# First batch's loads in written order, four weight tiles and two units' loads behind a copy to x, and other idle products, in a linear-attention and mixer kernel

## The chip, the cores and the metric

The kernel runs on one core of one Trainium2 chip. The metric is the device time of one execution in microseconds, the median of several runs. A core has a matrix engine (TensorE, here PE; its weight loads are shown apart as PEld), a vector engine (VectorE, DVE), an activation engine (ScalarE, ACT), a general engine (GpSimd, POOL) and a queue engine (SyncE, SP) that issues the DMA transfers. Each engine works through its own instructions in order; they wait for each other through semaphores.

## The reference

Two blocks follow each other. The first is a gated linear attention (hgrn2) over 4 batches, 8 heads, 768 steps and head dimension 48. The second is a token mixer of low rank and a channel mixer, on x of 4 x 768 x 384:

```python
f = 1.0 / (1.0 + np.exp(-f_logit))
state = np.zeros((B, H, D, D))
for t in range(S):
    state = f[:, :, t, :, None] * state + np.einsum('bhd,bhe->bhde', k[:, :, t], v[:, :, t])
    y[:, :, t] = np.einsum('bhd,bhde->bhe', q[:, :, t], state)
x = y.transpose(0, 2, 1, 3).reshape(B, S, H * D)
h = x.transpose(0, 2, 1) @ U @ V                 # U: 768 x 32, V: 32 x 768
u = x + h.transpose(0, 2, 1)
out = u + np.maximum(u @ w_ch1, 0.0) @ w_ch2     # w_ch1: 384 x 1536, w_ch2: 1536 x 384
```

q, k, v and f_logit are float32. The weights U, V, w_ch1 and w_ch2 come as float64, and the kernel turns them into float32 itself.

## The kernel before

The attention is cut into units of two heads: unit n is batch n // 4, head pair n % 4, so units 0 to 3 are the first batch. `factored_path` does the work; `general_path` behind it is compiled but not taken with these inputs. The sequence of a unit is cut into 12 chunks of 64 steps. A unit has a front (`prepare`: the logarithms or gates, the keys, the queries) and a rear (`attend`: `kept`, `spread`, `states`, `scan`, `scores`, `mask`, `read`, `inner`). `inner` ends with an ACT copy (L948) that puts the unit's 96 columns into `x_tiles[b]`. A mixer of a batch follows its attention (class `Mixer`); in the first batch the low-rank part is done in two pieces of columns: `done` holds the columns of units 0 to 2, `rest` those of unit 3.

The weights come in blocks of 128 x 384 words of 64 bits: `weights[0:3]` are U and V's two parts, `weights[3:15]` are the twelve blocks of w1, then twelve of w2. Each has a `start` (its DMA, L82), `halves` (two ACT instructions, L91 and L92) and `join` (three DVE instructions, L98 to L100, and an addition on POOL, L101). The first six blocks of w1 (`FIRST = 6`) land two by two in three tiles named zw, which `place` (L634) takes from the pool zp; those after them land in four rotating buffers named w_raw. A call of `loads[i]` starts a later block and converts block i.

The loads of q, k, v and f are issued by `load(n, ...)` on SP's queue (L544 to L572). Six issues fetch f, k and q of a unit of the first six, and three its v. Units up to 5 share two sets of buffers (`late` for even ones, `other` for odd), so that unit n + 2 waits for unit n's readers. A load's semaphore is one of eight used in turn.

What sets the order: PE's instructions stand as they are written, in the whole path. For the first batch and most of the second (L1026 to L1115) DVE and ACT do so as well; SP and POOL are in an order that the framework's scheduler makes. In that stretch the loop of L1043 runs over the four units of the first batch. It lists the pieces of unit n's rear, of unit n - 1's rear and of unit n + 1's front, calls them, and then issues loads: unit 3's f and unit 2's k, q, v and the first three weights after n = 0; unit 3's k, q, v and six blocks of w1 after n = 1; units 4 and 5 after n = 2 and 3. Three more weights follow at L1070. Behind the loop come the first mixer's low-rank products, from `low_rank_of(done)` (L1077) to `mix_of(rest)` (L1090), then `turn` (L261, the transposes of x, tile put) and `ch1` (L273, tile pz), the first large products. `ch1` writes one of two PSUM buffers, which an ACT relu (L283) frees.

Two helpers issue products whose results nobody reads: `busy(n)` (L1031) n products of 128 x 384, and `warm(n)` (L214) n products of 128 x 128. POOL fills `starts` (a plane of `other`) and both `fz` with zeros (L1093 to L1095); the second batch's gates need them.

Of the kernel before, what the change touches and what calls it, by code (L numbers as in the profile page):

```python
# [10 lines left out]
F32 = mybir.dt.float32  # L11
U32 = mybir.dt.uint32
U64 = mybir.dt.uint64
# [5 lines left out]
WP = 384  # L19
# [92 lines left out]
def ahead_by(n, loads):  # L112


    def call(i):
        if i + n < len(loads):
            loads[i + n][0]()
        loads[i][1]()

    return [lambda i=i: call(i) for i in range(len(loads))]  # L120
# [367 lines left out]
def factored_path(ctx, tc, q, k, v, f_logit, moe_U, moe_V, moe_w_ch1, moe_w_ch2, out, ok):  # L488
# [4 lines left out]
    nc = tc.nc  # L493
    B, H, S, D = q.shape
    P = nc.NUM_PARTITIONS
# [4 lines left out]
    HP = H // 2  # L500
# [4 lines left out]
    NFC = FF // P  # L505
# [17 lines left out]
    zp = ctx.enter_context(tc.tile_pool(name="zp", bufs=3))  # L523
# [21 lines left out]
    def load(n, *names):  # L545

        b, hp = divmod(n, HP)
        for nm in names:
            if nm == "v":
                v_tiles[n] = three.tile([P, NBL, 2, D], F32, name="v_nat")  # L550
            for par in range(2):
                head = src[nm][b, 2 * hp + par]
                if nm == "v" and par:

                    for s in range(2):
                        nc.sync.dma_start(
                            out=v_tiles[n][(1 - s) * C : (2 - s) * C, :, par, :],
                            in_=head.rearrange("(c s p) d -> s p c d", s=2, p=C)[s],
                        )
                    continue  # L560
                if nm == "v" or n < TURNED:
                    dst = v_tiles[n] if nm == "v" else nat[n % 2][nm]
                    nc.sync.dma_start(out=dst[:, :, par, 0:D], in_=head.rearrange("(c p) d -> p c d", p=P))
                    continue
                head = head.rearrange("(c i) d -> i c d", i=NB)
                for part in range(2):
                    p0 = par * PAD + part * NB
                    n_ch = min(NB, D - part * NB)
                    nc.sync.dma_start(  # L569
                        out=raw[n % 2][nm][p0 : p0 + NB, :].rearrange("p (c d) -> p c d", d=NB)[:, :, 0:n_ch],  # L570
                        in_=head[:, :, part * NB : part * NB + n_ch],
                    )  # L572
# [35 lines left out]
    starts = other[:, 3, :]  # L608
    fz = [const.tile([P, S + 1], F32, name=f"fz{i}") for i in range(2)]
# [17 lines left out]
    weights = [take_in(U, moe_U.rearrange("(c p) r -> p c r", p=P))]  # L627
    weights += [take_in(*pair) for pair in by_rows(V, moe_V, R)]
    early = len(weights)
    w1_rows = moe_w_ch1.rearrange("(c p) f -> p c f", p=P)  # L630

    spare = []
# [7 lines left out]
    FIRST = 6  # L640
# [128 lines left out]
    x_tiles = {}  # L769

    def mixer(b):
        return Mixer(tc, b, x_tiles[b], U, V, w1, w2, sums if b else None, ident, blocks, out, two, three, zp, ps_big, ps_mm,
                     b == 0, z_all, room if b >= B - 2 else None, FEWER - (b - B + 2) * NCH // 4)
# [184 lines left out]
    def front(n, *names):  # L958

        if n >= NU:  # L960
            return []
        if n not in ahead:
            ahead[n] = dict(zip(("gates", "keep", "keys", "read_back", "queries"), prepare(n)))
        return [ahead[n].pop(nm) for nm in names]

    def rear(n, *names):

        if not 0 <= n < NU:
            return []
        if n not in here:  # L970
            here[n] = dict(zip(("kept", "states", "scan", "scores", "read", "inner", "mask", "spread"), attend(n)))
        return [here[n].pop(nm) for nm in names if nm in here[n]]
# [9 lines left out]
    def steps(first, last):  # L982

        for n in range(first, last):
            yield from joined(rear(n - 2, "inner"), rear(n - 1, "scores"), rear(n, "kept"))
            if n + 1 < NU and n + 1 not in v_tiles:
                load(n + 1, "v")
            yield from front(n + 1, "gates", "keep", "keys")
            yield from joined(rear(n - 1, "read"), rear(n, "states", "scan"))
            yield from front(n + 1, "read_back", "queries")  # L990
            if n + 1 == last:
                yield from rear(n - 1, "inner")
                if n + 2 < NU:
                    load(n + 2, "v")

    def attention(pieces, portions, todo):

        fill = Fill(todo, portions)
        for piece in pieces:
            fill()  # L1000
            piece()
        fill.rest()
# [23 lines left out]
    with tc.manual_schedule(engines={nc.vector.engine, nc.scalar.engine}):  # L1026


        idle = ps_mm.tile([P, 512], F32, name="idle", tag="mm")

        def busy(n):  # L1031
            for _ in range(n):
                nc.tensor.matmul(idle[:, 0:DM], lhsT=ident, rhs=ends[:, 0:DM], start=True, stop=True)  # L1033

        busy(2)
        for piece in front(0, "gates", "read_back", "keep"):
            piece()
        load(2, "f")
        load(1, "k", "q", "v")
        loads = ahead_by(early + FIRST, weights)  # L1040
        halves, join = [[w[i] for w in weights[:early]] for i in (2, 3)]
        done, rest = slice(0, 2 * (HP - 1) * D), slice(2 * (HP - 1) * D, DM)
        for n in range(HP):  # L1043
            last = n + 1 == HP
            pieces = rear(n - 1, "scan", "mask") + front(n, "keys")
            if last:
                pieces += join[:1]
            elif n < 2:
                pieces += [lambda: busy(2)]
            pieces += rear(n, "spread") + rear(n - 1, "read") + rear(n, "kept")  # L1050
            if last:
                pieces += halves[1:2] + front(n, "queries") + rear(n - 1, "inner") + join[1:2] + rear(n, "states")
                pieces += halves[2:] + rear(n, "scores")
            else:
                pieces += rear(n - 1, "inner") + front(n + 1, "gates") + front(n, "queries") + rear(n, "states", "scores")
                pieces += (halves[:1] if n + 2 == HP else []) + front(n + 1, "read_back", "keep")
            for piece in pieces:
                piece()
            if n == 0:
                load(3, "f")  # L1060
                load(2, "k", "q", "v")
                for load_w in weights[:early]:
                    load_w[0]()
            elif n == 1:
                load(3, "k", "q", "v")
                for load_w in weights[early : early + FIRST]:
                    load_w[0]()
            else:
                load(n + 2, "f", "k", "q", "v")
        for load_w in weights[early + FIRST : early + FIRST + early]:  # L1070
            load_w[0]()

        m = mixer(0)
        low_rank_of, added_up_of, mix_of, warm = m.some
        for piece in rear(n, "scan", "mask") + join[2:]:
            piece()
        low_rank_of(done)  # L1077
        warm(2)
        loads[early]()
        for piece in rear(n, "read"):  # L1080
            piece()
        added_up_of(done)
        for piece in rear(n, "inner"):
            piece()
        mix_of(done, range(0, NBL - 2, 2))
        low_rank_of(rest)
        mix_of(done, range(NBL - 2, NBL, 2))
        added_up_of(rest)
        warm(2)
        mix_of(rest)  # L1090
        warm(2)
        loads[early + 1]()
        nc.gpsimd.memset(starts, 0.0)  # L1093
        for t in fz:
            nc.gpsimd.memset(t, 0.0)  # L1095
        loads = loads[early + 2 :]

        start = m.before[3:5] + m.firsts[0:1] + m.before[5:]

        EARLY = 6  # L1100
        second = chain(front(HP, "gates", "keep", "keys", "read_back", "queries"), steps(HP, 2 * HP + 1))
        for i, (_, piece) in enumerate(start + m.firsts[1:]):
            piece()
            if loads:
                loads.pop(0)()
            if i >= EARLY:
                next(second)()
        for f in loads:
            f()
        n = len(m.seconds) // (NBL // 2)  # L1110
        todo, after = m.seconds[:-n], m.seconds[-n:]

        attention(second, 12 + 10 * HP - (len(start) + len(m.firsts) - 1 - EARLY), todo)
        m = start_mixer(1, after)
        for f in to_sum:  # L1115
            f()
# [5 lines left out]
    pieces = beside(steps((B - 1) * HP + 1, NU + 1), 10 * (HP - 2), [lambda i=i: sum_of_w(i) for i in range(len(W_SUMS))])  # L1122
# [374 lines left out]
```

## Time and profile before

| | |
|---|---|
| runs | 488.84, 484.67, 487.88 us; median 487.88 |
| profiled execution, device time | 486.5 us |
| its span (first to last instruction) | 484.7 us |
| mean granted clock of TensorE over the span | 0.987 |
| busy: PE, PEld, DVE, ACT, POOL | 466.6, 402.8, 344.1, 179.8, 39.3 us |
| chain that ended last: PE, DVE, ACT, no releaser ("issue"), SP, DMA | 79%, 10%, 3%, 3%, 2%, 2% |

Times in the profile count from the span's first instruction. A line of a timeline has the start, the time taken, engine, source line, operation, tiles written and read, shape and count; in brackets stands the idle time of the engine before it and what ended it. A line of the chain has start, time and what ran; "issue" is time in which the engine waited for nothing that the profile shows. A line of a stage table has the stretch, its length, the busy time of PE, PEld, DVE, ACT and POOL with instruction counts, the granted clock of PE, the DMA engines' busy share and what they moved in GB/s. A product of float32 is recorded twice.

The stretch around the change ends at about 56 us, where the first product of `ch1` starts (56.05 us). From there to about 108 us PE is in `ch1` almost without a break, beside the second batch's first units.

### The profile page before, as it was taken

To read this page: it belongs to the slowest core of one execution; us is meant where nothing else is said; L and a number is where in the kernel's file an instruction comes from. 1 tells how busy PE (TensorE), PEld (TensorE's weight loads), DVE (VectorE), ACT (ScalarE), POOL (GpSimd) and SP (SyncE) were. 2 spreads that over 40 slices of the span, in tenths; PEclk is the share of its full clock that TensorE was granted. 3 is DMA by queue.
4 is the path that set the end of the run, shared out by engine and by line. 5 is a ranking of instruction groups with operands and counts; after the bars stand their busy time and mean duration, and the time that the engine had idled before them with its cause. 6 is when DMAs were issued, how large, how long until landed. Compare 5 with 4: busy or idle time off the path is not lost.

```text
span 484.7 us, 12802 instructions
## 1 busy us (share of the span) xinstructions
PE 466.6 (96%) x5563; PEld 402.8 (83%) x5563; DVE 344.1 (71%) x552; ACT 179.8 (37%) x333; POOL 39.3 (8%) x51
## 2 busy tenths in 40 slices
PE   6997999999999899999999999999999999999995
PEld 4885888886666468799899888899979999999995
DVE  2556579778999847666766655997896886858642
ACT  4683575664444313433342304543221311112200
POOL 3013145444000000000000000000000000000000
PEclk9998699999999999999999999999999999999999
DMA  9979975757687613152516300100000000000001
GB/s 145 158 163 245 182 186 132 162 144 93 102 122 114 102 41 43 26 74 50 85 26 108 50 16 18 28 3 20 17 1 1 33 2 18 18 0 34 1 33 40
DMA packets 158680, 34.36 MB, mean 71 GB/s; under 512 B 149206, under 2 KB 157078, under 8 KB 158614
## 3 DMA queue, kind: packets, MB, share of 16 engines
q1 hardware_dynamic: 158614, 33.44, 37.3%
q8 instruction: 46, 0.75, 0.7%
q14 instruction: 20, 0.16, 0.1%
HBM read 28.70 MB, written 4.72 MB: 69 GB/s over the span
## 4 chain that ended last, share of the span: by engine, by line
PE 79%; DVE 10%; ACT 3%; issue 3%; SPq 2%; DMA 2%; POOL 1%; DVEq 0%; POOLq 0%
PE pw L327 26%; PE pz L273 22%; PE pp L425 11%; PE sc L837 2%; PE y L942 2%; PE y L924 2%; PE put L261 2%; DVE late L759 2%; PE po L298 2%; PE pt L678 1%; PE pt L705 1%; DVE added L907 1%; SPq L569 1%; PE pt L864 1%; PE idle L1033 1%
## 5 line engine op out<-in xcount | busy, mean ns | idle before, releaser
L273 PE MATMUL pz<-uT,w 128*128 128x256 f32 x504 | 114.1, 382 | 1.1 <-ACT z_all L283 1.1
L273 PEld LDWEIGHTS pz<-uT,w 128*128 128x128 f32 x504 | 93.9, 190 | 14.3 <-ACT z_all L283 1.5
L327 PE MATMUL pw<-w,z_all 128*128 128x192 f32 x216 | 37.7, 329 | 0.0
L327 PE MATMUL pw<-zw,w_raw 128*128 128x192 f32 x216 | 37.3, 327 | 0.0
L327 PEld LDWEIGHTS pw<-zw,w_raw 128*128 128x128 f32 x216 | 35.2, 190 | 0.7 <-DVE w_raw L197 0.6
L327 PEld LDWEIGHTS pw<-w,z_all 128*128 128x128 f32 x216 | 35.0, 190 | 0.7
L101 POOL TENSOR_TENSOR w<-w_y,w_r 128x384 int32<-128x384 int32 x24 | 31.5, 1312 | 45.9 <-DVE w_y L100 38.6
L283 ACT ACTIVATE z_all<-pz 128x512 f32<-128x512 f32 x33 | 19.7, 597 | 34.6 <-PE pz L273 34.6
L425 PE MATMUL pp<-v_nat,late 128*128 128x128 f32 x224 | 28.8, 275 | 0.0
L425 PEld LDWEIGHTS pp<-v_nat,late 128*128 128x128 f32 x224 | 27.0, 192 | 0.0
L418 ACT ACTIVATE other<-other 128x512 f32<-128x512 f32 x18 | 11.3, 631 | 40.0 <-DVE other L197 40.0
L298 PE MATMUL po<-w,z_all 128*128 128x384 f32 x72 | 24.9, 493 | 1.2 <-DVE o L197 1.2
L912 ACT COPY st<-added 128x576 f32<-128x576 f32 x12 | 14.7, 1222 | 30.5 <-DVE added L907 30.5
L298 PE MATMUL po<-w,zw 128*128 128x384 f32 x72 | 25.3, 496 | 0.0
L741 DVE TENSOR_TENSOR_SCAN late<-fz,late 128x768 f32<-128x768 f32 x12 | 21.1, 1755 | 4.0 <-ACT fz L736 3.6
L850 DVE TENSOR_TENSOR A<-sc,causal 128x768 f32<-128x768 f32 x16 | 15.1, 945 | 10.5 <-PE sc L837 10.5
L298 PEld LDWEIGHTS po<-w,z_all 128*128 128x128 f32 x72 | 13.3, 190 | 10.1 <-DVE o L197 1.8
L298 PEld LDWEIGHTS po<-w,zw 128*128 128x128 f32 x72 | 13.1, 190 | 9.7 <-issue 1.2
L759 DVE TENSOR_TENSOR_SCAN late<-fz,other 128x768 f32<-128x768 f32 x12 | 21.0, 1747 | 0.2
L98 DVE TENSOR_SCALAR w_y<-w_y 128x384 f32<-128x384 f32 (+3 forms) x27 | 13.1, 487 | 10.6 <-ACT w_y L91 10.4
L197 DVE TENSOR_TENSOR x<-x,pu 128x768 f32<-128x768 f32 (+3 forms) x14 | 11.2, 835 | 12.9 <-PE pu L248 7.8
L924 PEld LDWEIGHTS y<-st,qT 48*64 48x64 f32 x704 | 13.7, 137 | 7.7 <-issue 5.4
(214 smaller groups left out, 855.0 us busy)
## 6 DMA issues: line engine op xcount, KB each, us to landing
w_raw<-in_moe_w_ch_dram SPq DMA_DIRECT2D x18, 384.0 KB, 3.5
out_dram<-o SPq DMA_DIRECT2D x24, 192.0 KB, 2.0
v_nat<-in_v_dram SPq DMA_DIRECT2D x16, 144.0 KB, 3.6
v_nat<-in_v_dram SPq DMA_DIRECT2D x32, 72.0 KB, 3.6
zw<-in_moe_w_ch_dram SPq DMA_DIRECT2D x6, 384.0 KB, 6.0
late<-in_f_logit_dram SPq DMA_DIRECT2D x10, 96.0 KB, 3.0
late<-in_k_dram SPq DMA_DIRECT2D x10, 96.0 KB, 2.7
late<-in_q_dram SPq DMA_DIRECT2D x10, 96.0 KB, 2.7
```

Source lines behind the costliest of these rows:

```text
L98: nc.vector.tensor_scalar(f, f, SMALLEST, LARGEST, ALU.max, ALU.min)
L101: nc.gpsimd.tensor_tensor(dst.bitcast(I32), shaped(y.bitcast(I32)), shaped(r), ALU.add)
L273: nc.tensor.matmul(pm[:, i * 2 * P : (i + 1) * 2 * P], lhsT=w1[:, m, o : o + P], rhs=uT[a][:, m, :], start=(m == 0), stop=(m == NDC - 1))
L283: nc.scalar.activation(z[a, c][:, k : k + 2, :].rearrange("p i t -> p (i t)"), pm, AF.Relu)
L298: nc.tensor.matmul(pm, lhsT=z[a, i // NI][:, i % NI, s * P : (s + 1) * P], rhs=w2[:, i, :], start=(i == 0), stop=(i == NFC - 1))
L327: nc.tensor.matmul(pm[:, n * HM : (n + 1) * HM], lhsT=lhs[:, i, :], rhs=rhs[:, i, :], start=(i == 0), stop=(i == NI - 1))
L425: nc.tensor.matmul(pm[:, i, r * P : (r + 1) * P], lhsT=room["w"](wn)[:, r * P : (r + 1) * P], rhs=x_node(a, xn), start=((xn, wn) == of[0]) ...
L741: nc.vector.tensor_tensor_scan(backwards(X, S - 1, S), backwards(f, S, S), backwards(ends, S - 1, S), 0.0, ALU.mult, ALU.add,)
L759: nc.vector.tensor_tensor_scan(Y, f[:, 0:S], starts, 0.0, ALU.mult, ALU.add)
L850: nc.vector.tensor_tensor(T["A"], sc[:, :, 0 : NBL * C].rearrange("p h (c i) -> p h c i", i=C), causal.unsqueeze(1).unsqueeze(1).broadcast ...
L912: nc.scalar.copy(st, states.rearrange(by_e, c=NCH))
L924: nc.tensor.matmul(o(c % 2, par, c // 2), lhsT=T["q"][rows[par], chunk[c]], rhs=T["st"][rows[par], c, :], start=(c <= 2), stop=False, skip ...
```

## The change

Five edits, all in `factored_path`:

- SP's instructions of the first batch stand in written order (`written`, closed behind the last loads of that stretch). The f of unit 2 thereby goes ahead of unit 1's k, q and v, and unit 3's f ahead of unit 2's.
- Only two of the six blocks of w1 are issued after n = 1. The other four are issued by `held`, called in the last iteration behind `rear(n - 1, "inner")`, the last copy but one to x. `held` takes the two zw tiles and has ACT copy one column of x into each, so that the DMAs into them cannot start before that copy; then it issues unit 4's loads.
- Unit 5's loads and the next three weights are issued behind the last conversion of V.
- `starts` and the two `fz` are filled by DVE behind the first block of w1, in place of POOL.
- `warm(2)` before `mix_of(rest)` is gone, and the one behind it is `warm(3)`.

In the changed program's order, v of unit 6 stands on SP behind unit 7's f, k and q; before it stood ahead of unit 6's f.

```diff
+        written = ExitStack()
+        written.enter_context(tc.manual_schedule(engines={nc.sync.engine}))
         busy(2)
...
+        def held():
+            for i in range(2, FIRST, 2):
+                t = zp.tile([P, NFC // 2, 2 * P], F32, name="zw").rearrange("p i t -> p (i t)")
+                nc.scalar.copy(t[:, 0:1], x_tiles[0][:, 0, 0:1])
+                spare.extend([t.bitcast(U64)[:, 0:WP], t.bitcast(U64)[:, WP : 2 * WP]])
+            for load_w in weights[early + 2 : early + FIRST]:
+                load_w[0]()
+            load(HP, "f", "k", "q", "v")
...
-                pieces += halves[1:2] + front(n, "queries") + rear(n - 1, "inner") + join[1:2] + rear(n, "states")
+                pieces += halves[1:2] + front(n, "queries") + rear(n - 1, "inner") + [held] + join[1:2] + rear(n, "states")
...
                 load(3, "k", "q", "v")
-                for load_w in weights[early : early + FIRST]:
+                for load_w in weights[early : early + 2]:
                     load_w[0]()
-            else:
-                load(n + 2, "f", "k", "q", "v")
-        for load_w in weights[early + FIRST : early + FIRST + early]:
-            load_w[0]()
...
         for piece in rear(n, "scan", "mask") + join[2:]:
             piece()
+        load(HP + 1, "f", "k", "q", "v")
+        for load_w in weights[early + FIRST : early + FIRST + early]:
+            load_w[0]()
+        written.close()
         low_rank_of(done)
         warm(2)
         loads[early]()
+        nc.vector.memset(starts, 0.0)
+        for t in fz:
+            nc.vector.memset(t, 0.0)
...
         added_up_of(rest)
-        warm(2)
         mix_of(rest)
-        warm(2)
+        warm(3)
         loads[early + 1]()
-        nc.gpsimd.memset(starts, 0.0)
-        for t in fz:
-            nc.gpsimd.memset(t, 0.0)
```

## The prediction

> **What bounds the kernel now.** I read the page's slices first. TensorE (PE) is near 96% busy, and its granted clock dips in one place only, the fifth slice, 48 to 61 us:
>
> ```profile
> PE   6997999999999899999999999999999999999995
> ...
> PEclk9998699999999999999999999999999999999999
> DMA  9979975757687613152516300100000000000001
> ```
>
> The change stays in the first 60 us (the first batch's attention, then the first mixer's low-rank part). So next comes the chain of waits there (start, us, what):
>
> ```profile
> 40.77 0.64 PE y L924 x18
> 41.41 2.01 issue
> 43.42 0.89 PE y L924 x24
> ...
> 53.79 2.33 PE put L261 x12
> 56.13 2.75 PE pz L273 x12
> ```
>
> Inside one run of equal products PE stops for 2.01 us with no releaser. Then the stage table (us, busy of PE, PEld, DVE, ACT, POOL, clock, DMA share, GB/s):
>
> ```profile
> 40.00:42.00 2.00, 1.35 (x22) 1.04 (x22) 1.90 (x6) 1.03 (x3) 0.51 (x2) 1.00 1.09 339
> 42.00:44.00 2.00, 0.58 (x25) 0.58 (x26) 0.74 (x2) 0.00 (x0) 1.00 (x1) 1.00 1.15 204
> 46.00:48.00 2.00, 2.00 (x22) 0.96 (x22) 0.70 (x2) 0.64 (x1) 0.00 (x0) 0.50 0.64 116
> 56.00:58.00 2.00, 2.00 (x11) 1.77 (x10) 1.30 (x4) 2.00 (x5) 0.12 (x1) 1.00 0.75 130
> ```
>
> DMA is full when PE stops, and from 45.52 to 55.76 us (the clock record) PE runs at half clock. That is why 12 transposes (put) take 2.33 us there; 18 take 1.97 at 178.92.
>
> The instruction packets on queue q8 tell the stop. [...] The one [...] starts at 41.10 and takes 1.12. In its way:
>
> ```profile
> 33.19 4.00 SPq L82 DMA_DIRECT2D zw<-in_moe_w_ch_dram  x6
> ```
>
> Six weight tiles of 384 KB, landing until 44.14. So the stage's bound is a late instruction fetch, then the slow clock behind it. From 59.5 to 108 us the chain is dense pz products, and from 113 to 168 it is DVE's; a gain at 56 us should travel through both.
>
> [...]
>
> **The change, part by part.** The sum is against the profiled execution: span 484.7, device time 486.5. The median of the three runs is 1.4 above that.
>
> *Four tiles held back.* Only two weight tiles now go out at 33.2; the other four wait in SP's queue for two ACT copies behind the x copy that ends at 37.70, so they issue from about 38.2 and move data from about 39.7 (issue to first landing is some 3 us). [...] the 2.01 stop goes.
>
> *The clock.* [...] Then I walk the chain at full-clock prices. y ends 41.9, ph 42.5 (0.68), y L942 43.4, eight pu 44.4, the x copy at 44.2 frees ph at 44.4, four pu 45.4, two ACT h copies (0.24 each) with ph between them 46.0, twelve pu 47.0, idle products 47.7. The last x additions (0.41 each) end at 48.0 and 48.4; then DVE's three steps of weight block 1 (0.36, 0.36, 0.56) 49.7, POOL's addition 50.7, first pz 50.75 instead of 56.05: **-5.3**, of which 2.0 is the stop.
>
> *Idle products.* Two pairs become one of three: two products fewer. The pair before mix_of(rest) cost 1.23 on the path (50.31 to 51.54); the three behind it hide under the additions and POOL's block 1. This is inside the -5.3. [...]
>
> *Memsets from POOL to DVE.* On POOL they ran at 4.03, 30.21 and 37.27 (to 38.02, before V's conversion at 38.58): their going gains nothing. On DVE three of 768 columns cost 0.70 each by this row, 2.1 in all, ahead of the x additions, where DVE now idles 4.53:
>
> ```profile
> 1.66 0.70 DVE L606 MEMSET late<- 128x768 f32 x1 [0.22 <-issue]
> ...
> 47.30 1.42 DVE L197 TENSOR_TENSOR x<-x,pu 128x576 f32<-128x576 f32 x2 [4.53 <-PE pu L248]
> ```
>
> With the stop gone the cover shrinks to about 1.5: DVE is free at 45.0 to 45.4 and the first additions are up to 1.0 late, but the last ones wait for PE at 47.0. Cost 0 to 0.5; I take 0.1.
>
> *Two ACT copies of one column*, about 0.15 each (the row of seen, L931, 0.15): added, the scan (1.36) and A shift by 0.3; y L924 had 0.9 of room behind the scan. Cost 0 to 0.3; I take 0.
>
> *Loads in written order.* f of unit 2 now stands before k and q of unit 1, and waits for unit 0's log sums (PE, 8.8 us); k and q (four issues), then v (three), are queued behind it. k of unit 1 landed at 13.60; two landings later (0.9 each) it is 15.4, just under its transposes at 15.59. q lands near 18.3, needed 20.17. f of unit 2 comes 4 us sooner, but DVE's 0.72 wait for it is not on the chain: ACT gets there only at 20.84, behind the x copy. The next batch of three swaps likewise with 1 us to spare. From -0.2 to +0.4; I take 0.
>
> *Behind the held tiles* on SP stand units 4 and 5 (f, k, q, v, nine issues each), then the weight tiles. DMA idles some 2 us at 38, and tile three lands about 0.9 later than its 40.36; all later loads shift by about that. The next weight block was issued at 55.84; it should land near 60.4. ACT reaches it 5.3 sooner than here:
>
> ```profile
> 63.20 0.58 ACT L91 ACTIVATE w_y<-w_raw 128x384 f32<-128x384 f32 x1 [0.45 <-POOL w L101]
> ```
>
> that is at 57.9, and waits 2.5. Behind it in ACT's order is a relu copy of pz that frees one of two PSUM buffers; PE has one more pz (2.6) to run, so little is passed on. v of unit 6 moves behind unit 7's loads (from 58.5 to about 110) and is needed at 127.7: nothing. From 0 to +2.5; I take +0.3.
>
> *The next fetch*, [...] now meets four tiles and f of unit 4. [...] No row shows it so placed: 0 to +2; I take +0.2.
>
> **Sum:** -5.3 +0.1 +0.3 +0.2 = -4.7: span 480.0, device 481.8, and with the median's 1.4 **483.2**. The shift has to live through the DVE stage to 168 us, whose order is unchanged.
>
> **The rivals.**
> (a) *Both stop and slow clock go* (forecast): 480.5 to 484.5. For: the fetch's lag stands alone among its neighbours and beside the tiles. Chance 0.52.
> (b) *Only the stop goes*: [...] Then the slow stretch costs its 3.3 again and the gain is 2.0 to 2.5: 485.5. Chance 0.16.
> (c) *Nothing*: the fetch is late for another reason (it lags as much with two tiles), or ACT's wait for the next weight block gives all back: 486.5 to 488.5. Against: two tiles are moved by 38. Chance 0.14.
> (d) *Slower*: [...] The stop of 2 to 3 comes back, and the half clock of 10.24 falls on dense pz products, where it costs 5.1 instead of 3.3; with the late weight block's 2.5 that is -5.3 +2.5 +5.1 +2.5 = +4.8 at worst, +3 in the middle: 491, up to 493. For: DMA is fuller there than now. [...] Chance 0.18.
>
> **How the numbers follow.** A measurement of this kernel tells about 1% from no change: 483.0 and 492.8. (a) straddles the lower bound; its small costs (+0.6 in all) are upper guesses, so I put 0.37 of its 0.52 below, and with the tail of (b), 0.03, faster is 0.40. Slower by over 1% is the far end of (d) and of the late weight block, 0.14; the rest, 0.46, is within 1%. The range 480.3 to 489 leaves out the ends of (a) and the upper half of (d).
>
> **What would show it.** Right: no "issue" of 2 us near 41; clock 1.00 throughout 10 to 60; the q8 packet near 37 to 39; first pz near 50.7; the first w_raw conversion on ACT ended by a DMA. Wrong: a stop of PE inside put; a clock of 0.50 anywhere from 45 to 70; pz later than 54; or an early gain that is gone by 108 or 168 us.

## The result, and the profile after

The changed kernel takes **484.09 us** (median of 20 runs, 482.98 to 485.23), the kernel before beside it 485.58 (20 runs, 482.35 to 488.84): a ratio of 0.996, 95% interval 0.994 to 0.998. That is within 1%, inside the forecast range, and 0.9 above the forecast of 483.2. The profiled execution has a span of 482.0 against 484.7 before, and 483.7 us of device time against 486.5. Medians are over all runs; two of the 22 runs of w_first_no_hold and two of hold_two's (both below) are slow, over 1.5% above the fastest of their kernel (the profiled execution of w_first_no_hold is one), and without them these two medians are 484.76 and 482.78.

The page's slices of the kernel after (PE's busy tenths, its granted clock, the DMA engines):

```profile
PE   6999989999999899999999999999999999999995
PEclk9999999999999999999999999999999999999999
DMA  9977985658787521153426200100000000000001
```

The dip of the clock in the fourth and fifth slice is gone. The chain of waits through the same stretch (start, us, what):

```profile
41.22 1.17 PE y L924 x43
42.39 0.68 PE ph L232 x2
...
47.48 0.86 PE ph L217 x6
48.35 0.67 PE put L261 x6
49.02 0.02 issue
49.04 0.81 ACT uT L262
49.85 0.14 issue
49.98 2.83 PE pz L273 x12
...
57.74 4.31 DMA w_raw<-in_moe_w_ch_dram
```

The y products run through in one piece: the stop of 2.01 us is gone, and the first pz starts at 49.98 instead of 56.05. But the chain then leaves PE and follows a weight block's DMA. The stage table (same columns as before) shows both ends:

```profile
40.00:42.00 2.00, 1.50 (x46) 1.37 (x46) 1.93 (x6) 1.30 (x3) 0.00 (x0) 1.00 0.74 213
42.00:44.00 2.00, 2.00 (x70) 1.44 (x66) 1.82 (x4) 0.58 (x3) 1.03 (x2) 1.00 1.02 333
46.00:48.00 2.00, 1.67 (x19) 1.41 (x19) 2.00 (x4) 1.13 (x3) 0.00 (x0) 1.00 0.77 144
...
62.00:64.00 2.00, 0.34 (x2) 0.32 (x3) 1.22 (x3) 1.87 (x5) 0.00 (x0) 1.00 1.09 351
```

From 42 to 44 PE is busy throughout (before: 0.58). From 62 to 64 it is busy for 0.34 of 2.00, where before had:

```profile
62.00:64.00 2.00, 2.00 (x11) 1.77 (x10) 1.93 (x5) 1.55 (x4) 0.99 (x1) 1.00 1.00 255
```

The timeline tells why:

```profile
57.74 6.76 SPq L82 DMA_DIRECT2D w_raw<-in_moe_w_ch_dram  x5
...
62.13 0.54 ACT L91 ACTIVATE w_y<-w_raw 128x384 f32<-128x384 f32 x1 [5.44 <-DMA w_raw<-in_moe_w_ch_dram]
...
63.66 5.45 PE L273 MATMUL pz<-uT,w 128*128 128x256 f32 x24 [1.76 <-ACT z_all L283]
...
73.31 2.86 PE L273 MATMUL pz<-uT,w 128*128 128x256 f32 x12 [0.96 <-ACT z_all L283]
```

ACT waits 5.44 us for the seventh block of w1. The relu of pz (L283, 63.02) stands behind that block's two conversions, so PE, with both PSUM buffers full, stops for 1.76. Because ACT is late, so are the second batch's gates on it (L728, 67.65) and DVE's scan behind them (L741, 70.76 to 72.51); the relu at 72.67 stands behind a copy that waits for the scan, and PE stops again for 0.96.

Against the kernel before, PE's work stands like this: first pz -6.07 us, the pz products up to 61 us the same, those at 66 us -4.04, from 76 us to the end -2.8. So **6.07 us were gained and 3.3 given back** between 61 and 76 us. The stage itself gained a little more: in this execution PE stood some 0.5 us behind before's from 9 to 38 us, its clock being full only from 9.12 us on (before: 7.97).

### The profile page after: what moved, and what is told of

Read it like the earlier page. It is cut to its first block, busy times and chain, and to the rows that moved or that the text cites. A ratio compares the mean times of both kernels' runs of the same rounds, so it can differ in the third digit from the quotient of the medians.

```text
span 482.0 us, 12801 instructions
## 1 busy us (share of the span) xinstructions
PE 462.7 (96%) x5561; PEld 399.8 (83%) x5561; DVE 345.3 (72%) x555; ACT 179.8 (37%) x335; POOL 36.3 (8%) x48
## 4 chain that ended last, share of the span: by engine, by line
PE 70%; DVE 13%; ACT 4%; DMA 4%; SPq 3%; issue 3%; POOL 1%; DVEq 0%; POOLq 0%; ACTq 0%
PE pw L327 26%; PE pz L273 16%; PE pp L425 12%; PE y L942 2%; DVE late L759 2%; PE sc L837 2%; PE y L924 2%; SPq L569 2%; PE po L298 2%; PE put L261 1%; PE pt L705 1%; DVE added L907 1%; PE pt L864 1%; PE idle L1033 1%; DVE late L741 1%
## 5 line engine op out<-in xcount | busy, mean ns | idle before, releaser
L283 ACT ACTIVATE z_all<-pz 128x512 f32<-128x512 f32 x33 | 19.7, 597 | 32.7 <-PE pz L273 32.6
L741 DVE TENSOR_TENSOR_SCAN late<-fz,late 128x768 f32<-128x768 f32 x12 | 21.1, 1756 | 4.0 <-ACT fz L736 3.6
L418 ACT ACTIVATE z_all<-z_all 128x512 f32<-128x512 f32 x12 | 7.6, 632 | 32.8 <-DVE z_all L197 32.8
L892 ACT COPY added<-ds 48x576 f32<-48x576 f32 (+1 forms) x28 | 17.8, 635 | 3.3 <-PE ds L885 3.2
```

What stands on the lines that cost most here:

```text
L283: nc.scalar.activation(z[a, c][:, k : k + 2, :].rearrange("p i t -> p (i t)"), pm, AF.Relu)
L418: nc.scalar.activation(dst, dst, AF.Relu, scale=float(SIGNS[n]))
L741: nc.vector.tensor_tensor_scan(backwards(X, S - 1, S), backwards(f, S, S), backwards(ends, S - 1, S), 0.0, ALU.mult, ALU.add,)
L892: nc.scalar.copy(added[r, 1:].rearrange("p (e c s) -> p e c s", c=NBL, s=2), ds[r, :, 0 : NBL * D].rearrange("p s (c e) -> p e c s", e=D),)
```

## The experiments

Fetch times below are the starts of the instruction packets on queue q8 (46 in before's trace, 0.75 MB) and count from the zero of the chain. On this zero the fetch that the prediction put at 41.10 stands at 40.80. The experiments were measured in three sets, each beside the kernel before, and the changed kernel only in the set of the result. The lowest runs of before in these four sets are 482.35, 482.74, 482.47 and 482.05, so a difference under about 0.7 us between sets is not read as an effect here. Medians of kernels that lose the clock differ more between sets (before: 485.58 to 487.60).

### What gives 3.3 us back

**w_first**: the three next weight blocks go ahead of unit 5's nine issues on SP.

```diff
-        load(HP + 1, "f", "k", "q", "v")
         for load_w in weights[early + FIRST : early + FIRST + early]:
             load_w[0]()
+        load(HP + 1, "f", "k", "q", "v")
         written.close()
```

> The changed kernel, with three weight blocks (six to eight of w1) issued ahead of unit 5's loads and no longer behind them. Theory A (the changed kernel gains 6.1 us at the first pz and gives 3.2 back because ACT waits 5.4 us for the next weight block's DMA): ACT's wait for w_raw near 57 to 62 us is under 1 us, PE has no stop of 1.8 us near 62, the first pz stays at 50 us, and the time falls by 2.5 to 3.2 us, to 481 (ratio to before 0.990). Theory B (the conversion chain of ACT, DVE and POOL is the limit there anyway, or unit 5's loads become late in turn): the time stays within 1 us of 484.1, and another wait ends where the DMA's ended.

Measured: 481.11 us (6 runs), ratio to before 0.989 (0.984 to 0.994). The first pz is at 49.76, and behind it, in the timeline:

```profile
56.94 0.57 ACT L91 ACTIVATE w_y<-w_raw 128x384 f32<-128x384 f32 x1 [0.46 <-POOL w L101]
...
66.62 0.56 ACT L91 ACTIVATE w_y<-w_raw 128x384 f32<-128x384 f32 x1 [1.42 <-DMA w_raw<-in_moe_w_ch_dram]
...
71.02 2.86 PE L273 MATMUL pz<-uT,w 128*128 128x256 f32 x12 [0.93 <-ACT z_all L283]
```

ACT's wait is no longer for the block but for POOL (0.46), and PE has no stop at 63. What is left is the fourth block, still issued behind unit 5: 1.42 on ACT, 0.93 on PE.

**f_first**: all four blocks ahead of unit 4's k, q, v and of unit 5.

```diff
             for load_w in weights[early + 2 : early + FIRST]:
                 load_w[0]()
-            load(HP, "f", "k", "q", "v")
+            load(HP, "f")
...
         for load_w in weights[early + FIRST : early + FIRST + early]:
             load_w[0]()
-        load(HP + 1, "f", "k", "q", "v")
-        written.close()
         low_rank_of(done)
         warm(2)
         loads[early]()
+        load(HP, "k", "q", "v")
+        load(HP + 1, "f", "k", "q", "v")
+        written.close()
```

> From w_first: SP's order behind the four held tiles is now f of unit 4, then all four weight blocks, then k, q, v of unit 4 and unit 5 (in w_first three blocks stand ahead of unit 5 and the fourth behind it). Theory A (the lateness of a weight block on SP's queue is the whole of what is given back after 60 us): ACT's 1.42 us wait for the fourth block at 66.6 us and PE's 0.93 us stop at 71.0 both go, first pz stays at 49.8, and the anchors behind 71 us come 0.8 to 1.1 earlier than in w_first: 480.0 to 480.5 against its 481.1. Rival B (k, q, v of units 4 and 5, now behind four blocks, become the late loads): the early gain is there at 75 us and is gone by 113 us, 481.0 to 482.0. Rival C (the fourth block waits for a buffer and not for the queue): nothing moves, 481.1.

Measured: 480.67 us (6 runs, 480.06 to 481.56), ratio 0.990 (0.986 to 0.994). In its timeline the fourth block is there in time and pz runs on:

```profile
65.12 0.56 ACT L91 ACTIVATE w_y<-w_raw 128x384 f32<-128x384 f32 x1
...
67.37 5.34 PE L273 MATMUL pz<-uT,w 128*128 128x256 f32 x24
...
72.56 0.82 PE L678 MATMUL pt<-ident,late 128*128 128x128 f32 x6
```

PE's work behind 73 us is 1.16 earlier than in w_first (expected 0.8 to 1.1), and that stays to the end of the span (478.3 against 479.6). The time lies just above theory A's 480.0 to 480.5 and below B's band. The transposes of the last line, which PE reaches at 76.00 in the changed kernel, stand 3.44 earlier here, 0.19 of it already there at the first pz. The rest, 3.25, is what the changed kernel gave back: it was the place of the weight blocks on SP's queue, all of it.

### What the stop and the half clock were

**no_hold**: the changed kernel with all six tiles issued after n = 1, as before. **w_first_no_hold**: the same on top of w_first.

```diff
-            for i in range(2, FIRST, 2):
...
-            for load_w in weights[early + 2 : early + FIRST]:
-                load_w[0]()
             load(HP, "f", "k", "q", "v")
...
-                for load_w in weights[early : early + 2]:
+                for load_w in weights[early : early + FIRST]:
```

> The changed kernel without holding: all six weight blocks are issued after unit 1's iteration, as before; loads in written order, DVE memsets and idle products stay changed. Theory A (the four tiles stood in the way of PE's instruction fetch): the stop of about 2 us without a releaser near 41 us is back in the profile[...]; clock 0.50 for 7 to 14 us behind it in the profile or in some runs; first pz at 54 us or later; time 485 to 487, with a wide spread. Theory B (idle products or the order of the loads took the stop away): no stop, first pz near 50, time 484 or less.

> Both edits together: six weight blocks at once, and the next three ahead of unit 5's loads. Theory A: the stop and its clock are back as without holding, so that the early weight blocks have little to save (ACT came late anyway): 484.5 to 487, some 4 us slower than with holding and early blocks. Theory B (the hold costs more through late loads than the stop does): faster than the kernel that holds and has the blocks early, 480.5 or less.

Measured: no_hold 485.31 us (14 runs), ratio 0.998 (0.995 to 1.001); w_first_no_hold 485.09 (22 runs), ratio 0.996 (0.993 to 0.999). The chain of no_hold:

```profile
41.65 0.64 PE y L924 x19
42.29 3.35 issue
45.64 0.98 PE y L924 x25
```

The stop is back, larger than before, and with it the half clock (44.14 to 50.97 us) and a late first pz (55.84). Against the changed kernel, in another set, no_hold's median is 1.2 higher, too little to tell. With the weight blocks in time, and in one set, the held tiles alone are worth 4.0 us of median (485.09 against w_first's 481.11). Four of the 22 runs of w_first_no_hold kept the clock (under 2 us of half clock, worked out as below): 481.12 to 483.24 us. So most of the 4.0 is the half clock; the stop alone comes to about 1 us (an estimate from these four runs).

**before_again**: the kernel before, unchanged, profiled once more.

> The kernel before once more, for its profile: its 20 runs lie from 482.35 to 488.84, the changed kernel's from 482.98 to 485.23. Theory A (the stop comes back in each execution[...]): a stop near 41 of 1.5 to 2.5 us, and clock 0.50 [...] at other times than 45.5 to 55.8. Theory B (the spread is of other origin): the same stop and the same half-clock stretch as in the first profile.

Measured: 484.56 us, span 482.7. The stop is there (2.10 us ahead of 43.95), but the half clock lasts 3.42 us only, from 45.52 to 48.94. The stage table:

```profile
44.00:46.00 2.00, 2.00 (x50) 1.49 (x52) 0.00 (x0) 0.56 (x2) 0.37 (x1) 0.88 0.95 157
46.00:48.00 2.00, 2.00 (x45) 1.31 (x40) 0.00 (x0) 0.64 (x1) 0.00 (x0) 0.50 0.56 105
48.00:50.00 2.00, 2.00 (x22) 1.10 (x18) 1.67 (x3) 0.24 (x1) 0.00 (x0) 0.77 1.15 207
```

The first pz is at 54.12 instead of 56.05. So the stop belongs to the program, and what follows from it differs from execution to execution.

**hold_two**: f_first with four tiles at 33 us and two held.

```diff
-            for i in range(2, FIRST, 2):
+            for i in range(4, FIRST, 2):
...
-            for load_w in weights[early + 2 : early + FIRST]:
+            for load_w in weights[early + 4 : early + FIRST]:
...
-                for load_w in weights[early : early + 2]:
+                for load_w in weights[early : early + 4]:
```

> f_first with two weight tiles held back instead of four: four go out at 33 us, one column copy on ACT instead of two. Theory A (the fetch waits for the tile bytes queued ahead of it, so its lag grows with the number of tiles): with six tiles ahead it started at 41.1 to 43.0, with two at 38.7 to 39.0; with four it should start at 39.8 to 41.0, PE's stop in the y products is 0 to 1.2 us, and the clock stays full or drops [...]. Time 480.5 to 483. Rival B (the fetch is late only when the whole backlog is there, an effect of the last tiles): it starts before 39.3, no stop, 480.2 to 481. Rival C (any backlog of more than two tiles holds it to its end): it starts at 41 or later, a stop of 2 us and more, and a half clock behind it: 483 to 486.

Measured: 483.53 us (22 runs, 480.81 to 488.17), ratio 0.996 (0.993 to 1.000). Its profiled execution kept the clock (481.21 us); its chain:

```profile
41.27 0.64 PE y L924 x19
41.91 0.72 issue
42.63 0.80 PE y L924 x25
```

In this trace the fetch starts at 40.02, between those behind two tiles and those behind six, as theory A has it. The time is not A's: its median lies above 480.5 to 483, because nine of the 22 runs lost the clock for over 9 us (below). The profiled executions with a stop, and three without, worked out from the traces:

| kernel | tiles sent at 33 us | fetch starts | PE goes on | between | stop | half clock |
|---|---|---|---|---|---|---|
| before | 6 | 40.80 | 43.42 | 2.62 | 2.01 | 45.52 to 55.76 |
| before_again | 6 | 41.44 | 43.95 | 2.51 | 2.10 | 45.52 to 48.94 |
| no_hold | 6 | 42.99 | 45.64 | 2.65 | 3.35 | 44.14 to 50.97 |
| w_first_no_hold | 6 | 42.14 | 44.63 | 2.49 | 2.17 | 44.80 to 58.45 |
| hold_two | 4 | 40.02 | 42.63 | 2.61 | 0.72 | none |
| after | 2 | 38.38 | | | none | none |
| w_first | 2 | 38.05 | | | none | none |
| f_first | 2 | 38.62 | | | none | none |

In the five with a stop, PE stops at the same place of its program and goes on 2.49 to 2.65 us after the fetch starts. That fixes the link from fetch to stop better than the one case of before could. By the same distances (an estimate) the changed kernel's fetch at 38.38 lets PE go on from near 41.0, and PE reaches the place (0.64 us into y) only at 41.86; in before the fetch at 40.80 is 0.61 us ahead of the stop at 41.41. A packet does not name the engine that it is for; that this one is PE's rests on this steady distance. The order by number of tiles rests on one execution of each kernel.

The half clock is the larger part of the loss, and the unsteady one. For 35 runs of the kernel before (w_first's set), I worked out from each run's mean clock how long it ran at half (1 minus the clock, times two, times the span; the clock's three decimals make this good to about 1 us, and some of it lies at the very end, where PE has little work: in before's trace from 482.43 us on, 2.3 us). It goes from 1.0 to 16.6 us, in steps, and the time follows it: correlation 0.95, 0.35 us for each us of half clock. The nineteen runs with more than 9 us have a median of 488.6, the nine with less than 5 of 484.7, the three with less than 2 lie from 482.7 to 483.5. These three lie below the changed kernel's median of 484.09, and in the result's own set before's two fastest runs (482.35, 482.43) lie below the changed kernel's fastest (482.98). An execution of before that keeps its clock is thus no slower than the changed kernel, which fits 3.3 given back against a stop of 2.0. What the change as it stands gains is the clock that it no longer loses. For hold_two it is the same as for before: half of its 22 runs kept the clock (under 4 us of half clock: 480.8 to 483.3), half lost it (483.7 to 488.2). The changed kernel never has more than 4.8 us in its 20 runs, which lie within 2.3 us.

### The small parts

All on top of w_first, since in the changed kernel itself ACT's wait until 62.13 covers small shifts ahead of it.

**w_first_two_pairs**: idle products as before, a pair ahead of `mix_of(rest)` and a pair behind.

```diff
+        warm(2)
         mix_of(rest)
-        warm(3)
+        warm(2)
```

> w_first with the idle products as in the kernel before (a pair ahead of the last mix_of and a pair behind it, instead of three behind it). Theory A (the removed pair lay on the path, at full clock 0.65 us for the two): first pz 0.3 to 0.7 later than w_first's 49.76, and the time 481.4 to 481.8. Rival B (PE waits for the additions to x there anyway, and the pair hides): first pz within 0.15 and the time within 0.2 of w_first's. Rival C (the idle pair is needed, or harmless, for the clock): no change of the granted clock is expected by A and B; C would show as a half clock in one of the two kernels between 45 and 60 us.

Measured: 481.25 us (11 runs). This execution stood 0.5 to 0.9 us later already ahead of the edit, so I count from the first L223 product behind the copy to x: the first pz comes 5.62 us later, in w_first 5.31. The pair costs **0.31** of path, at the lower end of theory A; the time stays below A's 481.4 and within B's 0.2 of w_first. Its timeline, first, and w_first's, second:

```profile
47.29 0.71 PE L217 MATMUL ph<-ident 128*128 128x128 f32 x4 [0.33 <-ACT h L233]
...
47.93 0.69 PE L248 MATMUL pu<-h,V 32*128 32x96 f32 x12
```

```profile
46.38 0.88 PE L248 MATMUL pu<-h,V 32*128 32x96 f32 x12 [0.33 <-ACT h L233]
```

The pair delays pu by 0.64, but pu then takes 0.69 instead of 0.88, and less idle work stands behind it. The first pz is 1.22 later than w_first's in all, and 0.70 of that is gone again at 71 us, where the wait for the fourth block shrinks (PE's stop is 0.22 instead of 0.93). The granted clock is 1.00 from 40 to 50 us in both, and 0.997 and 1.000 (w_first) over the whole of these executions, so C did not come.

**w_first_pool_memsets**: the three memsets back on POOL behind `warm(3)`.

```diff
-        nc.vector.memset(starts, 0.0)
-        for t in fz:
-            nc.vector.memset(t, 0.0)
...
         loads[early + 1]()
+        nc.gpsimd.memset(starts, 0.0)
+        for t in fz:
+            nc.gpsimd.memset(t, 0.0)
```

> w_first with the memsets back on POOL, behind the idle products, as in the kernel before. Theory A (DVE has room before the additions to x): the additions' last step and first pz move by less than 0.3 us either way, time within 0.3 of w_first's 481.1. Rival B (the 2.1 us on DVE delay the additions): first pz 0.3 to 1.0 earlier than 49.76, 480.2 to 480.8. Rival C (on POOL they stand before the rotation or the weight addition that the first pz needs): first pz 0.3 to 1.5 later, 481.4 to 482.6.

Measured: 481.75 us (11 runs, 480.78 to 482.59); the profiled execution is the lowest of them. In its trace the additions to x start at 44.63 instead of 45.39, pu takes 0.69 instead of 0.88, and the first pz comes 5.11 us after L223 instead of 5.31. On DVE the memsets cost 0.20 of path. The median says the opposite by 0.6, outside theory A's 0.3, so the same edit was put on f_first (**f_first_pool_memsets**):

> f_first with the memsets back on POOL behind the idle products. In the trace of w_first this move brought the additions to x 0.8 us forward and the first pz 0.2 us (counted from the x copy), but the medians of that call stood 0.6 above w_first's of another call. Theory A (the move is worth nothing or up to 0.3 on the path, and the median's difference was the spread of the calls): 480.2 to 480.8. Rival B (on POOL the memsets delay something behind 50 us in most executions, though not in the profiled one): 481.2 to 481.8.

Measured: 480.61 us (7 runs, 480.24 to 481.32), against f_first's 480.67. Nothing: theory A. Why w_first_pool_memsets' other ten runs lie higher stays open; it and w_first stand in different sets.

**w_first_old_order**: f of units 2 and 3 behind the k, q, v of units 1 and 2 again.

```diff
-        load(2, "f")
         load(1, "k", "q", "v")
+        load(2, "f")
...
-                load(3, "f")
                 load(2, "k", "q", "v")
+                load(3, "f")
```

> w_first with f of units 2 and 3 issued behind k, q, v of units 1 and 2, as in the kernel before. Theory A (the order of the first batch's loads costs and gains nothing): all PE anchors between 12 and 34 us within 0.1 us of w_first's [...], time within 0.2 of 481.1. Rival B (k and q of unit 1 behind the log sums of unit 0 were just late): up to 0.4 earlier than w_first. Rival C (f early helps the gates): up to 0.4 later.

Measured: 480.88 us (11 runs, 480.23 to 482.95), 0.23 from w_first. PE's work stands 0.40 behind w_first's from the start-up on, where its clock was full 0.9 us later (9.10 against 8.22), and 0.26 behind it from 23.65 us; from L223 to the first pz it takes 5.32 against 5.31. The one step between is w_first's and not the order's: its products of L837 take 1.06 us there, with a pause of 0.12 that ends 2.6 us after a fetch starts (20.27), and the changed kernel, in the new order too, takes 0.93 as this run does. That is theory A, with wider bounds than it gave itself.

The best of the ten are f_first and f_first_pool_memsets, 480.6 to 480.7 us: 1% below the kernel before, 0.7% below the changed one.

## Why the prediction was right, and where its sum was off

**The stop: right.** It was a late fetch of code behind weight tiles. In before's trace the packets on q8 ahead of it start at 14.81, 19.69, 24.38, 29.14 and 34.22, from 4.69 to 5.08 us apart, and the late one 6.58 behind the last of these. When it was due is not shown. With two tiles it came 2.42 us earlier (38.38), 4.90 behind the one ahead of it, and the stop went. Leaving out the hold alone brought it back (3.35), and four tiles gave a fetch at 40.02 and a stop of 0.72.

**The clock: right.** It stayed full to 480 us. That it would was an assumption, for no trace shows what the clock is granted by. And the half clock of before's profiled execution (10.24 us) is one case of several: another execution had 3.42 us, and in the three sets that have each run's clock, 19 of 35, 14 of 26 and 10 of 28 runs of before lost it for over 9 us. The 3.3 us that the sum took for it is the price of one trace. This fits that the 2.8 us between the profiles shrank to 1.5 between the medians, and that the offset of 1.4 from profile to median did not hold: over the 20 runs of the result, whose clocks are not on record, before's median is 485.58, below its profiled execution.

**The first pz: -6.07 instead of -5.3.** The term that failed is the last step of the walk, "POOL's addition 50.7, first pz 50.75". The first pz does not wait for the second weight block. In the chain above it follows put and ACT's copy uT, and it starts while POOL's addition is under way:

```profile
49.76 1.00 POOL L101 TENSOR_TENSOR w<-w_y,w_r 128x384 int32<-128x384 int32 x1 [5.34 <-DVE w_y L100]
...
49.98 2.83 PE L273 MATMUL pz<-uT,w 128*128 128x256 f32 x12 [0.33 <-ACT uT L262]
```

In w_first, too, it starts at 49.76 and the addition ends at 50.55.

**Memsets on DVE: 0.1 predicted, 0.20 measured** on the path. **Idle products:** the pair ahead of `mix_of(rest)` took 1.23 in before's trace at half clock; in w_first's place it costs 0.31. **ACT's two copies:** 0.29 together, at 38.10, no visible effect. **Written order: 0 predicted, nothing found.** **The next fetch: 0.2 predicted**, none measured: it started at 43.78, and PE did not stop in put.

**The late weight block: the mis-sized term, +0.3 predicted, 3.3 measured.** The mechanism and the place were named, and the range went to +2.5; the value taken was wrong. Three numbers make it up. The block was issued at 57.74 rather than about 56.8 (the prediction's 0.9 of shift on 55.84), and landed near 62.05 rather than 60.4. ACT was free at 56.69 rather than 57.9, since the stage ahead had shrunk by more. So the wait was 5.44 rather than 2.5. And "PE has one more pz to run, so little is passed on" is right for a wait of up to about 3.7 us at that place (5.44 less PE's stop of 1.76), but not for 5.4: 1.8 to 2.0 went to PE directly. The rest, 1.2, went through ACT's next pieces, as the second stop at 73.31 shows; this way is not in the prediction.

Of the rivals, (c)'s second half came true in part: ACT's wait gave back about half of the gain, not all. The slower case (d) did not come: the next fetch started at 43.78, and PE had no stop in put. That the forecast of 483.2 came within 0.9 of 484.09 is partly luck, for errors were opposed. In the profiled execution 0.8 more was gained ahead of 50 us, 3.0 more was given back, and the 0.3 for memsets and fetch did not show behind the first pz: 483.7 instead of 481.8. The median then lay 0.4 above the profiled execution instead of 1.4.

## What to carry to other kernels

When a stage gets shorter, walk the next stage with the new start times on every queue. Here holding four weight tiles back saved 6 us in one stage, and the first transfer that the next stage needs, at 56.7 us, stood behind eighteen issues of loads, the first of which PE used at 61 us. Order a queue by when the data are needed, not by which buffers come free first. And look at the clock of several executions before pricing a stretch at half clock: of two profiles of the kernel before, one shows 10.24 us of it and the other 3.42.

## What was not expected of the hardware

- A fetch of code started the later, the more weight tiles had been issued ahead of it (in one execution each): at 38.05 to 38.99 us with two tiles of 384 KB (seven kernels), at 40.02 with four, at 40.80 to 42.99 with six. The late ones stopped PE for 0.72 to 3.35 us.
- The stop can cost more through the clock than by itself. Behind stops of 2.01 to 3.35 us the traces of this stage show half clocks of 3.42, 6.83, 10.24 and 13.65 us; at 0.35 us for each us (the slope over the 35 runs above) that is 1.2 to 4.8 us, an estimate. How long it lasted differed between executions of one program.
- What the clock is granted by stays open. hold_two's profiled execution stopped for 0.72 us and kept the full clock, but nine of that kernel's 22 runs were at half clock for over 9 us.
